# Letting a list scheduler choose each engine's instruction order in a speech-model kernel

## The chip, the cores and the metric

The kernel runs on one core of a Trainium2 chip. The metric is the device time of one execution in microseconds (us). Every kernel here was executed several times beside the kernel before on the same chip. "Ratio" below is the mean time of one kernel's fast runs over the mean of the fast runs of the kernel before in the same rounds, with a 95% interval; so it is not quite the ratio of the medians that are quoted. The kernel gives each of five engines its own sequence of instructions: TensorE (PE, matmuls; PEld is its weight load), VectorE (DVE), ScalarE (ACT), GpSimd (POOL) and SyncE (SP, which issues loads and stores). The kernel makes the engines wait for each other through semaphores.

## The reference

Two strided convolutions with 5 taps, each followed by GELU, then a joint layer (B=2, T=4000, D=512, K=5, U=8):

```python
for i in range(K):
    h = h + einsum("btc,cd->btd", xp[:, i:i+T, :], w1[i])
h = gelu(h)[:, ::2, :]
... the same with w2 on h, giving f[:, ::2, :]        # 1000 frames of each batch
fe = einsum("btd,de->bte", f, w_f);  ge = einsum("bud,de->bue", g, w_g)
j  = tanh(fe[:, :, None, :] + ge[:, None, :, :])
return einsum("btud,dv->btuv", j, w_o)                # (2, 1000, 8, 512)
```

## The kernel before

It is already well tuned: the convolutions use fewer products than the plain form by adding and subtracting inputs and weights first. So TensorE needs *operands* that VectorE and ScalarE make. These are sums and differences of shifted frames (`xt`, `row`, and `xs`, `hT` in place) and of weights (`w_t`). The products are then combined by VectorE (`scalar_tensor_tensor`, in the accumulator `acc` or in `ty`, `sd`), and a ScalarE GELU follows. The frames go through in five tiles of the first convolution, two batches of the second (`Triple`, 4 units each), and then 125 output tiles of 128 rows.

Every operation is recorded once, in program order, and each engine gets its own operations in that order:

```python
for o in ops:                       # program order
    if o.eng != name: continue
    for k, v in o.deps.items(): wait(...)      # latest conflicting op of each other engine
    ins = o.fn(e)
```

The order was placed by hand, as lists of which preparation step follows which product:

```python
LATE = {(0, 0): ((1, "2d"), (0, "next"), (0, "ti"), (0, "t0"), (0, "s0")), (0, 1): ((1, "r"),), ...}
...
def unit(self, m, vec=(), scal=()):            # one output block of a tile
    ... three products; then, in the accumulator:
    for o, f in ((C, 0.5), (Dd, -0.5)):
        stt("dve", ps.cols(o, n), ps.cols(Dd, n), f, c)
    ends.append(end)       # four more products into the same accumulator, then GELU
    finish(2 if m else 1)  # the ends are run one or two units later
```

## Time and profile before

The kernel takes 298.3 us (median of 3; 298.7 with a fourth run).

From the page of the kernel before: span, busy time by engine, rows of busy tenths in 40 slices of the span, and the chain of waits by engine.

```profile
span 296.9 us, 4003 instructions
...
PE 273.6 (92%) x1474; PEld 144.6 (49%) x1486; DVE 188.2 (63%) x282; ACT 172.8 (58%) x220; POOL 1.6 (1%) x18
...
PE   8998699999989959876979869999999999999995
...
DVE  1999956654976973099474322566766767666674
...
PEclk9999799999999989979999979999999999999999
...
PE 66%; DVE 15%; SPq 5%; ACT 5%; DMA 5%; issue 3%; DVEq 0%; ACTq 0%
```

In the PE row the dips lie in slices 5 to 24, so at about 30 to 175 us; from there on, in the output stage, PE never stops. The PEclk row (TensorE's granted clock, in tenths) has four dips that follow the deeper dips of PE. No other engine is near 100% over the span.

The waits of PE in the kernel before: who was waited for, total us, times, longest us.

```profile
PE acc L305 <- DVE hT L294: 3.9, 3, 2.8
PE acc L305 <- ACT jT L298: 3.5, 1, 3.5
PE acc L305 <- DVE acc L447: 2.9, 1, 2.9
PE acc L305 <- issue: 2.7, 1, 2.7
PE acc L305 <- DVE row L294: 2.4, 1, 2.4
PE acc L305 <- DVE feT L778: 1.5, 1, 1.5
...
```

A few long stops, then, not many short ones. What was ahead of the missing operand is seen on the other engines. The timeline of ScalarE of the kernel before, at 121 to 126 us (start, length, engine, line, operation, out<-in, shapes, count, and in brackets the idle time before it and what ended it):

```profile
121.18 3.64 ACT L298 ACTIVATE row<-hT 128x1344 bf16<-128x1344 bf16 x2
124.72 1.30 ACT L298 ACTIVATE row<-row 128x1336 bf16<-128x1336 bf16 x1
```

The timeline of VectorE of the kernel before, just after it:

```profile
126.06 1.62 DVE L294 TENSOR_TENSOR row<-row 128x1336 bf16<-128x1336 bf16 x2 [11.26 <-ACT row L298]
```

The timeline of TensorE of the kernel before, where it waits for that:

```profile
127.74 0.74 PE L305 MATMUL acc<-row,w_sb 128*128 128x334 bf16 x4 [2.37 <-DVE row L294]
```

The copy at 124.72 is what VectorE waits for, and behind VectorE TensorE. It belongs to the first batch. Its input had been there since 103.5 us (end of VectorE's subtract into `row`), but in the list above it stands behind two copies of the second batch, whose input was ready only at 120.7 (end of the last GELU of their tile). So VectorE slept for 11.3 us over a 1.3 us copy.

The half clock is seen in the timeline of TensorE of the kernel before, after the stop of 2.89 us at 29.6 us; four matmuls of 498 columns take 1.87 us in the half-clock stretch and 1.00 us later:

```profile
34.92 1.87 PE L305 MATMUL acc<-xs,w_t 128*128 128x498 bf16 x4
...
41.87 1.00 PE L305 MATMUL acc<-xs,w_t 128*128 128x498 bf16 x4
```

### The profile page before, as it was taken

Reading aid. Unit: us, or ns where it says so; the run is one execution under the profiler, and the core shown is the slowest. Engines: PE = TensorE matmul, PEld = TensorE weight load, DVE = VectorE, ACT = ScalarE, POOL = GpSimd, SP = SyncE. Lnnn points to the kernel's source line nnn. Section 1 sums busy time; section 2 is a strip of 40 time slices with the busy share of each in tenths; the row PEclk is TensorE's granted clock in tenths of the full one; section 3 lists DMA queues with packets and bytes.
Section 4 is the critical chain, followed back from the end, with each engine's and each line's share of the span. In section 5 each row is a group of like instructions: output and inputs, shape, how many; then the busy total and the mean of one; then the engine's idle time right before and its main releaser. Section 6 shows DMA issues by size and latency. Waiting matters only on the chain.

```text
span 296.9 us, 4003 instructions
## 1 busy us (share of the span) xinstructions
PE 273.6 (92%) x1474; PEld 144.6 (49%) x1486; DVE 188.2 (63%) x282; ACT 172.8 (58%) x220; POOL 1.6 (1%) x18
## 2 busy tenths in 40 slices
PE   8998699999989959876979869999999999999995
PEld 4896364444444425544645535444444444444442
DVE  1999956654976973099474322566766767666674
ACT  2758647229328531835442865295976786884941
POOL 1000000000000000000000000000000000000000
PEclk9999799999999989979999979999999999999999
DMA  7999989960000000000000011134444454444444
GB/s 268 279 174 219 203 186 244 348 137 1 2 0 0 2 0 0 0 2 1 0 0 2 0 35 55 53 106 161 145 148 162 135 176 145 156 155 148 159 145 141
DMA packets 54721, 31.87 MB, mean 107 GB/s; under 512 B 31646, under 2 KB 54446, under 8 KB 54702
## 3 DMA queue, kind: packets, MB, share of 16 engines
q1 hardware_dynamic: 54558, 31.55, 38.9%
q8 instruction: 12, 0.20, 0.3%
q10 hardware_dynamic: 144, 0.07, 0.1%
q14 instruction: 7, 0.06, 0.1%
HBM read 7.86 MB, written 16.38 MB: 82 GB/s over the span
## 4 chain that ended last, share of the span: by engine, by line
PE 66%; DVE 15%; SPq 5%; ACT 5%; DMA 5%; issue 3%; DVEq 0%; ACTq 0%
PE acc L305 66%; SPq L337 5%; DVE acc L447 4%; DVE row L294 2%; DMA xs<-in_x_dram 2%; ACT row L298 2%; DVE hT L294 2%; DVE sd L447 2%; DMA w_sb<-in_w_dram 2%; DVE xt L294 1%; DMA xr<-in_x_dram 1%; ACT fT L298 1%; ACT hT L298 1%; DVE xs L294 1%; DVE w_t L294 1%
## 5 line engine op out<-in xcount | busy, mean ns | idle before, releaser
L305 PE MATMUL acc<-wo_sb,jT 128*128 128x512 bf16 (+1 forms) x492 | 109.3, 381 | 4.1 <-ACT jT L298 3.5
L864 DVE CAST ost<-acc 128x512 bf16<-128x512 f32 (+1 forms) x105 | 72.3, 689 | 45.5 <-PE acc L305 45.5
L305 PEld LDWEIGHTS acc<-wo_sb,jT 128*128 128x128 bf16 x504 | 49.7, 99 | 63.2 <-ACT jT L298 3.6
L298 ACT ACTIVATE jT<-feT,geT 128x1000 bf16<-128x1000 f32 (+5 forms) x84 | 70.9, 918 | 0.0
L305 PE MATMUL acc<-xt,w_sb 128*128 128x252 bf16 (+2 forms) x240 | 46.2, 335 | 3.0 <-DVE acc L447 2.9
L298 ACT ACTIVATE hT<-acc 128x996 bf16<-128x996 f32 (+2 forms) x16 | 14.4, 899 | 35.0 <-PE acc L305 35.0
L305 PEld LDWEIGHTS acc<-xt,w_sb 128*128 128x128 bf16 x240 | 23.6, 99 | 20.9 <-ACT cs L298 3.1
L305 PE MATMUL acc<-xs,w_t 128*128 128x498 bf16 (+2 forms) x140 | 30.8, 349 | 1.4 <-DVE xs L294 0.8
L298 ACT ACTIVATE ost<-acc 128x512 bf16<-128x512 f32 (+1 forms) x21 | 12.3, 584 | 29.8 <-PE acc L305 29.8
L447 DVE SCALAR_TENSOR_TENSOR acc<-acc,cs 128x498 f32<-128x498 f32 (+2 forms) x30 | 17.5, 629 | 17.5 <-PE acc L305 10.7
L298 ACT ACTIVATE xt<-xs 128x1992 bf16<-128x1992 bf16 (+2 forms) x14 | 21.6, 1572 | 3.3 <-DMA xs<-in_x_dram 3.3
L305 PE MATMUL acc<-row,w_sb 128*128 128x334 bf16 x96 | 18.7, 320 | 5.1 <-issue 2.7
L305 PE MATMUL acc<-hT,w_t 128*128 128x334 bf16 x96 | 17.2, 317 | 3.9 <-DVE hT L294 3.9
L305 PEld LDWEIGHTS acc<-xs,w_t 128*128 128x128 bf16 x140 | 13.4, 99 | 13.6 <-DVE xs L294 1.5
L305 PE MATMUL acc<-xs,w_sb 128*128 128x252 bf16 (+2 forms) x104 | 19.7, 322 | 0.1
L298 ACT ACTIVATE cs<-acc 128x498 f32<-128x498 f32 (+3 forms) x27 | 12.9, 486 | 10.6 <-PE acc L305 8.5
L298 ACT ACTIVATE fT<-acc 128x334 bf16<-128x334 f32 (+1 forms) x16 | 11.6, 727 | 11.8 <-PE acc L305 11.6
L305 PE MATMUL acc<-xt,w_t 128*128 128x252 bf16 (+2 forms) x88 | 17.4, 329 | 0.0
L294 DVE TENSOR_TENSOR row<-row 128x1336 bf16<-128x1336 bf16 x8 | 6.5, 850 | 16.4 <-ACT row L298 16.4
L305 PE MATMUL acc<-fT,wf_sb 128*128 128x500 bf16 x64 | 14.0, 374 | 1.5 <-DVE feT L778 1.5
L305 PEld LDWEIGHTS acc<-row,w_sb 128*128 128x128 bf16 x96 | 9.5, 101 | 11.0 <-issue 3.1
L294 DVE TENSOR_TENSOR xt<-xt,xs 128x1992 bf16<-128x1992 bf16 (+2 forms) x14 | 14.0, 1011 | 0.4 <-ACT xt L298 0.4
(55 smaller groups left out, 198.4 us busy)
## 6 DMA issues: line engine op xcount, KB each, us to landing
out_dram<-ost SPq DMA_DIRECT2D x109, 128.0 KB, 1.9
w_sb<-in_w_dram SPq DMA_DIRECT2D x10, 512.0 KB, 5.5
xr<-in_x_dram SPq DMA_DIRECT2D x2, 512.0 KB, 3.8
wg_sb<-in_w_g_dram SPq DMA_DIRECT2D x1, 512.0 KB, 10.1
wf_sb<-in_w_f_dram SPq DMA_DIRECT2D x1, 512.0 KB, 6.9
wo_sb<-in_w_o_dram SPq DMA_DIRECT2D x1, 512.0 KB, 7.7
xs<-in_x_dram SPq DMA_TRANSPOSE x16, 4.9
out_dram<-ost SPq DMA_DIRECT2D x2, 120.0 KB
```

Source lines behind the costliest of these rows:

```text
L294: pl.op(eng, lambda e: e.tensor_tensor(out=o.ap, in0=a.ap, in1=b.ap, op=op), (a, b), (o,))
L298: pl.op("act", lambda e: e.activation(o.ap, i.ap, func, scale=scale, bias=0.0 if bias is None else bias.ap), rd, (o,))
L305: ins = e.matmul(o.ap, lhsT=l.ap, rhs=r.ap, start=start and n == 0, stop=stop and n == len(pairs) - 1, skip_group_check=not check)
L337: pl.dma("sp", lambda e: e.dma_start_transpose(out=dst.ap, in_=src), (), (dst,))
L447: pl.op(eng, lambda e: e.scalar_tensor_tensor(out=o.ap, in0=a.ap, scalar=f, in1=b.ap, op0=ALU.mult, op1=add), (a, b), (o,))
L864: pl.op("dve", lambda e, o=o, v=v: e.tensor_copy(out=o.ap, in_=v.ap), (v,), (o,))
```

## The change

Its intent is that instruction order is no longer written by hand but computed at build time: a list scheduler walks through simulated time with a cost for each operation and a model of the loads, and each engine takes an operation that is ready. On VectorE and ScalarE it is the one that TensorE will need soonest (`late`, worked out backwards from TensorE's own sequence). On TensorE, SyncE and GpSimd it is the first in program order of those that are ready, so TensorE too may go round a product whose operands aren't there. The result is a fixed order per engine. The opening, up to the second tile's operands, stays pinned to program order. Three further outputs of the second tile are moved from `unit` to the form that keeps its sums apart (`whole` and `post`), which costs an extra VectorE add each.

```diff
+    def edges(self):      # all pairs of ops that touch the same bytes or PSUM bank
+    ...
+    def schedule(self, pred):
+        for i in range(n - 1, -1, -1):
+            t = min([late[s] - (HOP if pred[s][i] else ...) for s in succ[i]], default=0.0)
+            if ops[i].eng == "pe":
+                t = min(t, nextpe)
+            late[i] = t - span[i]
+    ...
+            now = [i for i in cand[e] if ready[i] <= t + 0.02]
+            i = min(now, key=(lambda i: i) if e in ("pe", "sp", "pool") else (lambda i: (late[i], i)))
+    ...
+            if o.dma:
+                wire = max(wire, t + 1.0) + o.nbytes / 222e3
+                end = max(wire, t + 2.0)
 ...
-            for o in ops:
-                if o.eng != name:
-                    continue
+            for i in order[name]:
 ...
+        def vec_cost(o, ins, fast=True):
+            return o.ap.free_size() * (0.52e-3 if bf else 1.04e-3) + 0.065
 ...
-        post0(1)
-        post0(2, (lambda: tiles[2].shift("a0"),))
-        post0(3)
-        tiles[2].xf("a0")
-        t1.post(0, t1.whole(0), (lambda: tiles[2].shift("b1"),))
-        tiles[2].xf("a1")
+        pl.pin = False
+        for m in base0:
+            post0(m)
+        ... all operands of the third tile
+        for m in range(WHOLE):          # 4; was 1
+            t1.post(m, t1.whole(m))
```

No matmul, load, store or eviction is added or saved, apart from the three adds.

More of the change, by code (lines that the diff above doesn't have):

```diff
@@ L63 @@
 class Op:
-    __slots__ = ("eng", "fn", "deps", "dma", "signal", "count", "sem", "val", "idx")
+    __slots__ = ("eng", "fn", "reads", "writes", "dma", "signal", "count", "sem", "val", "idx", "cost", "pin", "after", "nbytes")
 class Plan:
     COMPUTE = ("pe", "act", "dve", "pool")
+    HOP = 0.16
     def __init__(self, nc):
@@ L74, in __init__ @@
         self.ops = []
-        ncell = 229376 // CELL + 1
-        z = lambda n: {e: np.full(n, -1, np.int64) for e in self.COMPUTE + ("dma",)}
-        self.lw, self.lr, self.pa = z(ncell), z(ncell), z(8)
-    def _deps(self, eng, reads, writes):
-        need = {}
-        def add(e, arr, cells):
-            m = int(arr[cells].max())
-            if m >= 0:
-                if e == "dma":
-                    for d in set(arr[cells].tolist()):
-                        if d >= 0:
-                            need[("dma", d)] = True
-                else:
-                    need[e] = max(need.get(e, -1), m)
-        for v in list(reads) + list(writes):
-            if v.psum:
-                for e in self.COMPUTE:
-                    if e != eng:
-                        add(e, self.pa[e], v.cells)
-        for v in reads:
-            if not v.psum:
-                for e in self.lw:
-                    if not (e == eng == "pe"):
-                        add(e, self.lw[e], v.cells)
-        for v in writes:
-            if not v.psum:
-                for e in self.lw:
-                    if not (e == eng == "pe"):
-                        add(e, self.lw[e], v.cells)
-                        add(e, self.lr[e], v.cells)
-        return need
@@ L110, in op @@
-    def op(self, eng, fn, reads=(), writes=()):
+        self.pin = True
+    def op(self, eng, fn, reads=(), writes=(), cost=0.1):
         o = Op()
         o.eng, o.fn, o.dma, o.signal, o.idx = eng, fn, False, False, len(self.ops)
-        o.deps = self._deps(eng, reads, writes)
+        o.reads, o.writes, o.cost, o.pin, o.after = tuple(reads), tuple(writes), cost, self.pin, []
         self.ops.append(o)
-        for v in list(reads) + list(writes):
-            if v.psum:
-                self.pa[eng][v.cells] = o.idx
-        for v in reads:
-            if not v.psum:
-                self.lr[eng][v.cells] = o.idx
-        for v in writes:
-            if not v.psum:
-                self.lw[eng][v.cells] = o.idx
@@ L124, in op, with dma @@
         return o
-    def dma(self, eng, fn, reads=(), writes=(), sem=None):
+    def dma(self, eng, fn, reads=(), writes=(), sem=None, nbytes=524288):
         o = Op()
         o.eng, o.fn, o.dma, o.signal, o.idx = eng, fn, True, False, len(self.ops)
-        o.deps = self._deps("dma_issue", reads, writes)
+        o.reads, o.writes, o.cost, o.pin, o.after, o.nbytes = tuple(reads), tuple(writes), 0.05, True, [], nbytes
         if sem is None:
@@ L135, in dma @@
         self.ops.append(o)
-        for v in reads:
-            self.lr["dma"][v.cells] = o.idx
-        for v in writes:
-            self.lw["dma"][v.cells] = o.idx
-        return o
+        return o
+    def edges(self):
+        ops = self.ops
+        sets, label = {}, {False: np.zeros(229376 // CELL + 1, np.int64), True: np.arange(8)}
+        for o in ops:
+            for v in o.reads + o.writes:
+                k = (v.psum, v.cells.tobytes())
+                if k not in sets:
+                    sets[k] = v.cells
+                    if not v.psum:
+                        lab = label[False]
+                        lab[v.cells] += lab.max() + 1
+                        label[False] = np.unique(lab, return_inverse=True)[1]
+        na = int(label[False].max()) + 1
+        atoms = {k: (np.unique(label[k[0]][c]) + (na if k[0] else 0)) for k, c in sets.items()}
+        R = np.zeros((len(ops), na + 8), np.float32)
+        W = np.zeros_like(R)
+        for o in ops:
+            for m, vs in ((R, o.reads), (W, o.writes)):
+                for v in vs:
+                    m[o.idx, atoms[(v.psum, v.cells.tobytes())]] = 1
+        sb = slice(0, na)
+        hit = lambda s: (W[:, s] @ (R + W)[:, s].T + R[:, s] @ W[:, s].T) > 0
+        sbuf, psum = hit(sb), hit(slice(na, na + 8))
+        pred = []
+        last = {}
+        for o in ops:
+            p = {}
+            for j in np.flatnonzero(sbuf[o.idx, :o.idx] | psum[o.idx, :o.idx]).tolist():
+                q = ops[j]
+                if o.dma and q.dma and not set(x for v in o.writes for x in v.cells.tolist()) & set(
+                        x for v in q.reads + q.writes for x in v.cells.tolist()):
+                    continue
+                same = q.eng == o.eng and not q.dma and not o.dma
+                over = any(W[o.idx, c] > R[o.idx, c] and R[j, c] + W[j, c] > 0 for c in range(na, na + 8))
+                p[j] = not same or (bool(sbuf[o.idx, j] or over) and o.eng != "pe")
+            for j in o.after:
+                p[j] = True
+            if o.pin:
+                j = last.get(o.eng)
+                if j is not None:
+                    p.setdefault(j, False)
+                last[o.eng] = o.idx
+            pred.append(p)
+        return pred
@@ new lines, in schedule @@
+    def schedule(self, pred):
+        ops, HOP = self.ops, self.HOP
+        n = len(ops)
+        succ = [[] for _ in ops]
+        for i, p in enumerate(pred):
+            for j in p:
+                succ[j].append(i)
+        span = [o.cost + (4.0 if o.dma else 0.0) for o in ops]
+        late, nextpe = [0.0] * n, 0.0
+        for i in range(n - 1, -1, -1):
+            t = min([late[s] - (HOP if pred[s][i] else ops[i].cost - span[i]) for s in succ[i]], default=0.0)
+            if ops[i].eng == "pe":
+                t = min(t, nextpe)
+            late[i] = t - span[i]
+            if ops[i].eng == "pe":
+                nextpe = late[i]
+        left = [len(p) for p in pred]
+        ready = [0.0] * n
+        free = {e: 0.0 for e in ("pe", "act", "dve", "pool", "sp")}
+        cand = {e: [] for e in free}
+        for i in range(n):
+            if not left[i]:
+                cand[ops[i].eng].append(i)
+        order = {e: [] for e in free}
+        wire, start = 0.0, [0.0] * n
+        for _ in range(n):
+            best = None
+            for e, c in cand.items():
+                if c:
+                    t = max(free[e], min(ready[i] for i in c))
+                    if best is None or t < best[0]:
+                        best = (t, e)
+            t, e = best
+            now = [i for i in cand[e] if ready[i] <= t + 0.02]
+            i = min(now, key=(lambda i: i) if e in ("pe", "sp", "pool") else (lambda i: (late[i], i)))
+            cand[e].remove(i)
+            order[e].append(i)
+            o = ops[i]
+            start[i] = t
+            free[e] = t + o.cost
+            end = free[e]
+            if o.dma:
+                wire = max(wire, t + 1.0) + o.nbytes / 222e3
+                end = max(wire, t + 2.0)
+            for s in succ[i]:
+                ready[s] = max(ready[s], end + HOP if pred[s][i] else free[e])
+                left[s] -= 1
+                if not left[s]:
+                    cand[ops[s].eng].append(s)
+        self.start = start
+        self.end = max(free.values())
+        return order
@@ L142, in emit @@
     def emit(self, block, tail):
         nc, ops = self.nc, self.ops
+        pred = self.edges()
+        order = self.schedule(pred)
+        pos = {i: p for e in order for p, i in enumerate(order[e])}
+        deps = []
         for o in ops:
-            for k, v in o.deps.items():
+            need = {}
+            for j, w in pred[o.idx].items():
+                q = ops[j]
+                if not w:
+                    continue
+                if q.dma:
+                    need[("dma", j)] = j
+                elif q.eng not in need or pos[need[q.eng]] < pos[j]:
+                    need[q.eng] = j
+            deps.append(need)
+            for k, j in need.items():
@@ L146, in emit @@
                 if not isinstance(k, tuple):
-                    ops[v].signal = True
+                    ops[j].signal = True
         cnt = {e: 0 for e in self.COMPUTE}
         sem = {e: nc.alloc_semaphore(f"s_{e}") for e in self.COMPUTE}
-        for o in ops:
-            if not o.dma:
-                if o.signal:
-                    cnt[o.eng] += 1
-                o.count = cnt[o.eng]
+        for e in self.COMPUTE:
+            for i in order[e]:
+                if not ops[i].dma:
+                    if ops[i].signal:
+                        cnt[e] += 1
+                    ops[i].count = cnt[e]
@@ L162, in wait @@
                     e.wait_ge(s, v)
-            for o in ops:
-                if o.eng != name:
-                    continue
-                for k, v in o.deps.items():
+            for i in order[name]:
+                o = ops[i]
+                for k, j in sorted(deps[i].items(), key=lambda kj: -kj[1]):
                     if isinstance(k, tuple):
-                        wait(ops[k[1]].sem, ops[k[1]].val)
+                        wait(ops[j].sem, ops[j].val)
                     else:
-                        wait(sem[k], ops[v].count)
+                        wait(sem[k], ops[j].count)
                 ins = o.fn(e)
@@ L237, in bass_standalone__seq2seq_rnn_t_joint__speech_kernel @@
     NWARM = 10
+    WHOLE = 4
     with ExitStack() as es:
@@ L288, in bass_standalone__seq2seq_rnn_t_joint__speech_kernel @@
         sub, add = ALU.subtract, ALU.add
+        def vec_cost(o, ins, fast=True):
+            bf = fast and all(not v.psum and v.ap.dtype == BF16 for v in (o,) + tuple(ins))
+            return o.ap.free_size() * (0.52e-3 if bf else 1.04e-3) + 0.065
         def memset(v):
@@ L293, in tt @@
         def tt(eng, o, a, b, op):
-            pl.op(eng, lambda e: e.tensor_tensor(out=o.ap, in0=a.ap, in1=b.ap, op=op), (a, b), (o,))
+            pl.op(eng, lambda e: e.tensor_tensor(out=o.ap, in0=a.ap, in1=b.ap, op=op), (a, b), (o,),
+                  vec_cost(o, (a, b)))
         def act(o, i, func, scale=1.0, bias=None):
@@ L298, in act @@
             pl.op("act", lambda e: e.activation(o.ap, i.ap, func, scale=scale,
-                                                bias=0.0 if bias is None else bias.ap), rd, (o,))
+                                                bias=0.0 if bias is None else bias.ap), rd, (o,),
+                  o.ap.free_size() * 0.83e-3 + 0.11)
         def mm(o, pairs, start, stop, check=True):
@@ L307, in fn @@
                 return ins
-            pl.op("pe", fn, [v for pr in pairs for v in pr], (o,))
+            pl.op("pe", fn, [v for pr in pairs for v in pr], (o,), len(pairs) * max(o.ap.free_size() / 2400 + 0.0025, 0.1))
         zv = zero[:]
@@ L344, in load_w1 @@
             if after is not None:
-                o.deps[("dma", after.idx)] = True
+                o.after.append(after.idx)
             return o
@@ L374, in fn @@
                     return ins
-                pl.op("pe", fn, (xr[rt][:], ident[:]), (pv,))
+                pl.op("pe", fn, (xr[rt][:], ident[:]), (pv,), 0.8)
                 o = xs[0][pp::2, :, 16 + rt * P:16 + (rt + 1) * P]
@@ L379, in bass_standalone__seq2seq_rnn_t_joint__speech_kernel @@
                 else:
-                    pl.op("dve", lambda e, o=o, pv=pv: e.tensor_copy(out=o.ap, in_=pv.ap), (pv,), (o,))
+                    pl.op("dve", lambda e, o=o, pv=pv: e.tensor_copy(out=o.ap, in_=pv.ap), (pv,), (o,), vec_cost(o, (pv,)))
         def shift(src, off, dst, c0, n, which):
@@ L447, in stt @@
             pl.op(eng, lambda e: e.scalar_tensor_tensor(
-                out=o.ap, in0=a.ap, scalar=f, in1=b.ap, op0=ALU.mult, op1=add), (a, b), (o,))
+                out=o.ap, in0=a.ap, scalar=f, in1=b.ap, op0=ALU.mult, op1=add), (a, b), (o,),
+                  vec_cost(o, (a, b), False))
         def w2part(m, part):
@@ L735, in bass_standalone__seq2seq_rnn_t_joint__speech_kernel @@
         t1.xf("a3")
-        post0(1)
-        post0(2, (lambda: tiles[2].shift("a0"),))
-        post0(3)
-        tiles[2].xf("a0")
-        t1.post(0, t1.whole(0), (lambda: tiles[2].shift("b1"),))
-        tiles[2].xf("a1")
+        pl.pin = False
+        for m in base0:
+            post0(m)
+        nxt = tiles[2]
+        nxt.shift("a0")
+        nxt.xf("a0")
+        nxt.shift("b1")
+        nxt.xf("a1")
+        nxt.shift("a3")
+        for w in ("a2", "b1", "b3", "a3"):
+            nxt.xf(w)
+        for m in range(WHOLE):
+            t1.post(m, t1.whole(m))
         flush()
@@ L777, in fe @@
                     else:
-                        pl.op("dve", lambda e, o=o, v=v: e.tensor_copy(out=o.ap, in_=v.ap), (v,), (o,))
+                        pl.op("dve", lambda e, o=o, v=v: e.tensor_copy(out=o.ap, in_=v.ap), (v,), (o,), vec_cost(o, (v,)))
         def tanh(v, k):
@@ L805, in bass_standalone__seq2seq_rnn_t_joint__speech_kernel @@
             nx = tiles[qi + 1] if qi + 1 < len(tiles) else None
-            for m in range(1 if qi == 1 else 0, NK):
+            for m in range(WHOLE if qi == 1 else 0, NK):
                 if qi == 1:
-                    scal = ((), ("a3",), (), ())[m]
-                    vec = ((), ("a2", "b1"), ("b3", "a3"), ())[m]
+                    scal, vec = (), ()
                 elif nx:
@@ L863, in bass_standalone__seq2seq_rnn_t_joint__speech_kernel @@
                 else:
-                    pl.op("dve", lambda e, o=o, v=v: e.tensor_copy(out=o.ap, in_=v.ap), (v,), (o,))
+                    pl.op("dve", lambda e, o=o, v=v: e.tensor_copy(out=o.ap, in_=v.ap), (v,), (o,), vec_cost(o, (v,)))
                 lo = c0
@@ L871, in bass_standalone__seq2seq_rnn_t_joint__speech_kernel @@
                     dst = out[b, t:t + n, u, cl]
-                    pl.dma(("sp", "act")[h], lambda e, src=src, dst=dst: e.dma_start(dst, src.ap), (src,), (), slot_sem[s])
+                    pl.dma(("sp", "act")[h], lambda e, src=src, dst=dst: e.dma_start(dst, src.ap), (src,), (), slot_sem[s], 2 * n * P * 4)
                     lo += n
```

## The prediction

> **What bounds the kernel now.** TensorE. The page shows PE 92% busy (273.6 of 296.9 us); the chain of waits has 66% on PE. The output stage (from 173 us) is gapless in the timeline: nothing is to be had there. What a reordering can win lies between 24 and 173 us, where PE stands still though its operands could have been made earlier. The PE timeline shows these idle stretches: 2.9 us at 29.6 (vector work of the second tile's units), 0.8 at 81.7 (a subtract queued behind weight sums), 2.7 + 0.8 at 105 to 109, 2.4 at 125.3 and 2.8 + 0.3 at 137.7 to 142 (operands of the second convolution), 1.5 at 154 (feT evictions), 3.5 at 169.5 (first tanh rows). With crumbs at 24 to 29 that is about 19 us.
>
> **The clock.** After four of them (29.6, 105, 125, 169.5) matmuls run at half speed for about 3.4 us (498 columns take 0.41 us between starts instead of 0.21; granted clock 0.83 in 30 to 40 us). [...] Each costs 1.7 us, together 7. Removable in all: about 25 us.
>
> **Order or data?** Mostly order. VectorE is 69% busy from 40 to 110 us, ScalarE less. At 126 VectorE had waited 11.3 us for a ScalarE copy standing behind the other batch's copies (3.6 us). The tanhs at 165 to 173 use feT that was ready at 160. The scheduler puts what TensorE needs soonest first, and lets PE take whichever product is ready. What it can't lift: 20 to 40 us, where VectorE is busy 19.4 of 20 us and x arrives until 30.8; and the second convolution, where VectorE needs 2.4 us per unit and 10 us of operands per batch against 5.0 us of PE per unit, nearly as much as PE, and the second batch's operands can't start before their buffer is free at 119.7.
>
> **Added.** Three more outputs of the second tile take the separate path: each adds a 504-column add (0.68 us), 2 us of VectorE in its fullest stage, but PE then needn't wait for VectorE in mid-accumulation. The scheduler's costs are 10 to 20% below the trace (0.60 against 0.69 us for 512 f32 on VectorE; 0.94 against 1.12 for a tanh), and it counts the half-size loads of x as full ones, so it expects x some 5 us late and puts other work ahead. New small PE gaps will come of this. No matmul or byte is saved.
>
> **Sum (gain, with clock).** 24 to 40 us: 3.5 of 6.5; 81: 0.7; 105: 4.5 of 5.1; 125: 3.5 of 4.1; 138: 1.5 of 3.1; 154: 1; 169: 4.5 of 5.2. That is 19; less 1.5 for new gaps: 17.5.
>
> **Predicted: 280.8 us, 274 to 290 in 8 of 10. Faster by over 2%: 0.91; within 2%: 0.07; slower: 0.02.**
>
> **What would show it.** PE busy falls to 265 to 272 us (less half clock) while its share rises to 95% or more. The dips of the PE clock row near 33, 108, 129 and 173 us go, at most one staying. The output stage keeps its length and starts about 17 us sooner. PE's waits for jT and row vanish; one for VectorE near 22 to 35 us remains.
>
> **What would make it wrong.** A static order from wrong costs can stall in-order engines: VectorE behind a late product, or tanhs ahead of an eviction in the output stage. If the second convolution is truly bound by VectorE, 125 to 140 gains little and the time is near 288.

## The result and the profile after

The changed kernel takes 273.5 us (median of 4; 273.3 to 274.2) against 298.7 us: ratio 0.9172 (0.9132 to 0.9212). It is 25.1 us faster; 17.5 had been predicted, and the time lies just below the stated range.

From the page of the changed kernel, the same lines:

```profile
span 271.7 us, 3949 instructions
...
PE 265.2 (98%) x1474; PEld 142.7 (53%) x1486; DVE 188.5 (69%) x285; ACT 173.6 (64%) x220; POOL 1.6 (1%) x18
...
PE   8899999999999999999999999999999999999995
...
DVE  1899999829999952699544354666667656657764
...
PEclk9999999999999999999999999999999999999999
...
PE 87%; ACT 6%; DMA 4%; issue 1%; SPq 0%; DVE 0%
```

The dips are gone from both the PE row and the clock row. VectorE does the same work (188.5 against 188.2 us), only sooner: its row is now at 8 or 9 tenths in slices 2 to 8 and 10 to 14, where it had holes in slices 6 to 10, 12 and 13; one hole is left, in slice 9. All that is left of PE's waits:

```profile
PE acc L383 <- DVE zero L390: 1.2, 1, 1.2
PE acc L383 <- DVE xt L370: 0.7, 1, 0.7
PE acc L383 <- ACT fT L375: 0.6, 1, 0.6
PE acc L383 <- ACT hT L375: 0.3, 1, 0.3
```

Two of these are in the pinned opening (the first at the very start, the 0.7 us at 7.2 us); between 20 us and the end PE stands still for 0.8 us. The copy that had been queued wrongly now runs soon after the two copies (and the subtract) that it depends on, 35.7 us earlier in the run; in the timeline of ScalarE of the changed kernel:

```profile
81.75 3.65 ACT L375 ACTIVATE row<-hT 128x2688 bf16<-128x2688 bf16 x2
...
89.04 1.31 ACT L375 ACTIVATE row<-row 128x1336 bf16<-128x1336 bf16 x1
...
109.96 3.65 ACT L375 ACTIVATE row<-hT 128x2688 bf16<-128x2688 bf16 x2
```

The copies of the second batch follow at 109.96, when their input exists.

The account of the 25.2 us between the two spans (all sums worked out from the PE timelines and the clock records; PE idle is without the 3.1 us after the last matmul, the same in both):

| | before | after | difference |
|---|---|---|---|
| PE idle, all | 20.3 | 3.5 | 16.8 |
| half-clock stretches (four of 3.41 us, less 0.55 us of a stop that lies in one; half of the rest is lost) | 6.5 | 0 | 6.5 |
| rest (PE's busy time) | | | 1.9 |

Part of the rest is most likely the end of the last matmul before a stop, which the trace counts as busy: a group of four 498-column matmuls ends 1.00 us after its start, but the next group starts 0.84 us after it when there is one, so each stop hides about 0.16 us more. There are ten stops before and three after, so that is 1.1 us of the 1.9. This is an estimate from those two numbers and was not tested; the other 0.8 us is not accounted for. The output stage, from its fourth tile on, is as long as before: the span between the second block of output matmuls (181.65 us before, 156.41 after) and the last matmul (293.9 and 268.7) is 112.2 us in both.

### The profile page after: what moved, and what is told of

Same layout as the page of the kernel before. It is cut to its first block, busy times and chain, and to the rows that moved or that the text cites. A ratio compares the mean times of both kernels' runs of the same rounds, so it can differ in the third digit from the quotient of the medians.

```text
span 271.7 us, 3949 instructions
## 1 busy us (share of the span) xinstructions
PE 265.2 (98%) x1474; PEld 142.7 (53%) x1486; DVE 188.5 (69%) x285; ACT 173.6 (64%) x220; POOL 1.6 (1%) x18
## 4 chain that ended last, share of the span: by engine, by line
PE 87%; ACT 6%; DMA 4%; issue 1%; SPq 0%; DVE 0%
PE acc L383 87%; DMA w_sb<-in_w_dram 4%; ACT jT L375 3%; ACT fT L375 1%; ACT cs L375 0%; ACT xt L375 0%; ACT feT L375 0%; SPq L407 0%; DVE feT L864 0%; ACT hT L375 0%; ACT ost L375 0%
## 5 line engine op out<-in xcount | busy, mean ns | idle before, releaser
L383 PE MATMUL acc<-wo_sb,jT 128*128 128x512 bf16 (+1 forms) x492 | 107.8, 377 | 1.2 <-ACT fT L375 0.6
L375 ACT ACTIVATE jT<-feT,geT 128x1000 bf16<-128x1000 f32 (+10 forms) x84 | 72.1, 922 | 17.9 <-PE acc L383 16.9
L383 PE MATMUL acc<-xs,w_t 128*128 128x498 bf16 (+2 forms) x140 | 29.5, 341 | 0.0
L375 ACT ACTIVATE hT<-acc 128x996 bf16<-128x996 f32 (+2 forms) x13 | 12.6, 967 | 21.0 <-PE acc L383 21.0
L525 DVE SCALAR_TENSOR_TENSOR sd<-acc,cs 128x334 f32<-128x334 f32 x16 | 7.4, 500 | 18.3 <-PE acc L383 15.3
L383 PEld LDWEIGHTS acc<-xs,w_t 128*128 128x128 bf16 x140 | 13.6, 98 | 10.9
L383 PE MATMUL acc<-row,w_sb 128*128 128x334 bf16 x96 | 17.5, 305 | 0.0
L383 PE MATMUL acc<-hT,w_t 128*128 128x334 bf16 x96 | 16.3, 305 | 0.0
L525 DVE SCALAR_TENSOR_TENSOR acc<-acc,cs 128x498 f32<-128x498 f32 (+1 forms) x24 | 15.3, 678 | 0.8 <-PE acc L383 0.8
L383 PEld LDWEIGHTS acc<-xs,w_sb 128*128 128x128 bf16 x104 | 10.0, 98 | 7.2 <-DVE xs L458 0.9
```

What stands on the lines that cost most here:

```text
L375: pl.op("act", lambda e: e.activation(o.ap, i.ap, func, scale=scale, bias=0.0 if bias is None else bias.ap), rd, (o,), o.ap.free_size() * ...
L383: ins = e.matmul(o.ap, lhsT=l.ap, rhs=r.ap, start=start and n == 0, stop=stop and n == len(pairs) - 1, skip_group_check=not check)
L525: pl.op(eng, lambda e: e.scalar_tensor_tensor(out=o.ap, in0=a.ap, scalar=f, in1=b.ap, op0=ALU.mult, op1=add), (a, b), (o,), vec_cost(o, (a ...
```

## The experiments

In all of them the numbers to compare with are 273.5 us and ratio 0.9172 for the changed kernel, and 298.4 to 299.2 us for the kernel before. All 15 gave correct results.

### Which engine's freedom does it?

Four kernels with the program text of before, built by the new class. `HOLD` lists the engines that stay in program order:

```diff
+    HOLD = ("pe", "act", "dve", "pool")      # old_all_held; 3, 1 or 0 of them in the others
-        ... cost, self.pin, []
+        ... cost, self.pin or eng in self.HOLD, []
```

> Program text of before (second tile mostly by in-place units), with the new dependence bookkeeping, but every engine held to program order. Theory (the gain is order): within 1.5 us of before, about 298. Rival (the new pairwise dependences drop waits that the old bookkeeping had): below 293.

Measured: 298.5 us, ratio 1.003 (0.997 to 1.008). The new bookkeeping of dependences by itself is worth nothing. PE stops at the same ten places.

> As old_all_held, but TensorE alone is freely ordered; VectorE, ScalarE and GpSimd stay in program order. Theory (the operands come late because VectorE and ScalarE make them in the wrong order): little gain, 293 to 297. Rival (TensorE taking whatever product is ready fills its own gaps): below 285.

Measured: 279.6 us, ratio 0.937 (0.933 to 0.942). The theory fell: TensorE's own freedom gives three quarters of the gain, with VectorE and ScalarE in the old order. Its PE waits for VectorE and ScalarE after the start sum to 5.4 us, and no half-clock stretch is left within the work of the profiled run (two of the other three executions have a mean clock of 0.993 to 0.994, so probably one stretch). The old 3.5 us wait for the first tanh rows is gone because PE now does most of the last products of the second convolution in that time, which the old text had placed behind the third output tile. The first output matmuls in the timeline of TensorE of the kernel before:

```profile
173.05 4.22 PE L305 MATMUL acc<-wo_sb,jT 128*128 128x512 bf16 x11 [3.51 <-ACT jT L298]
177.11 0.73 PE L305 MATMUL acc<-row,w_sb 128*128 128x334 bf16 x4
```

The same in the timeline of old_pe_free, with products of the second convolution right before them:

```profile
157.55 0.73 PE L383 MATMUL acc<-hT,w_sb 128*128 128x334 bf16 x4
158.17 2.76 PE L383 MATMUL acc<-wo_sb,jT 128*128 128x512 bf16 x12
```

> TensorE held to program order; VectorE, ScalarE and GpSimd freely ordered. Theory: most of the gain, 277 to 284, what is missing lies at 24 to 40 us. Rival (TensorE's own choice does it): 290 or more.

Measured: 277.5 us, ratio 0.930 (0.927 to 0.933). As expected. What is missing lies at 21 to 37 us: small stops for VectorE of 0.2 to 1.3 us and, in the profiled run (278.2 us, clock 0.994), one half-clock stretch. The other three executions have a clock of 1.000 and take 277.3 to 277.5 us, so most of the median's distance is the stops.

> All engines freely ordered, program text of before, so the changed kernel without its three further separate outputs of the second tile. Theory: 275 to 278, the separate outputs are worth 2 to 4 us at 24 to 40 us because TensorE then need not wait for VectorE in mid-accumulation. Rival (the scheduler alone does all): within 1 us of the changed kernel, 273.5.

Measured: 274.5 us, ratio 0.920 (0.917 to 0.923). This is within 1 us of the changed kernel, and the intervals overlap, so the three further separate outputs are worth at most about 1 us, not 2 to 4; the trace shows 0.7 us of stops at 22 to 26 us that the changed kernel hasn't.

What follows: the two freedoms are substitutes. Singly they gain 18.8 and 21 us, together 24. A stop of PE goes away when the operand comes sooner, or when PE has something else that is ready; here one of the two was mostly enough.

### Does urgency matter?

```diff
-            i = min(now, key=(lambda i: i) if e in ("pe", "sp", "pool") else (lambda i: (late[i], i)))
+            i = min(now, key=lambda i: i)
```

> The changed kernel, but VectorE and ScalarE take the ready instruction that is first in program order, as TensorE does; the urgency is not used. Theory A (urgency towards TensorE is what fills the gaps): 277 to 283. Theory B (after the first four runs: either side's freedom is enough, so any order by readiness does): within 1.5 us of the changed kernel, below 275.

Measured: 274.5 us, ratio 0.920 (0.917 to 0.924). Theory B: taking the first ready operation in program order does nearly as well; the difference of 0.3% is inside the intervals. "Ready" is what counts here, "most urgent" adds at most about 1 us. Not tested is how much of the gain moving the few misplaced steps by hand would have brought.

### How good must the cost model be?

The prediction deducted 1.5 us for errors of the scheduler's costs. `true_cost` mends them; the three flat kernels make them much worse.

```diff
 # true_cost
-            return o.ap.free_size() * (0.52e-3 if bf else 1.04e-3) + 0.065
+            return o.ap.free_size() * (0.52e-3 if bf else 1.04e-3) + 0.155
-                  o.ap.free_size() * 0.83e-3 + 0.11)
+                  o.ap.free_size() * 0.83e-3 + (0.28 if bias is not None else 0.17))
 # loads of x: nbytes = (hi - lo) * 1024 instead of 524288 for all
 # flat_cost: both of these; flat_compute: the first alone; flat_load: the second alone
+        for o in ops:
+            if not o.dma: o.cost = 0.7
+            else:         o.nbytes = 0
```

> The changed kernel, with the scheduler's costs of VectorE and ScalarE raised to the durations of the trace (0.69 us for 512 f32, 1.11 for a tanh of 1000) and the loads of x counted at their true size. The prediction held 1.5 us for gaps that wrong costs make: ratio to the changed kernel 0.994. Rival (TensorE stands only 0.8 us between 21 and 268 us, so nothing is left): within 0.3% of the changed kernel, 273 to 274.

Measured: 273.2 us, ratio 0.916 (0.913 to 0.919). Nothing beyond noise. The errors that the prediction listed (10 to 20% on VectorE and ScalarE, 5 us on the loads of x) cost next to nothing.

> The changed kernel, but the scheduler believes that every compute instruction and group of matmuls takes 0.7 us and every load lands 2 us after issue. Theory A (the order is only as good as its cost model, as the prediction feared): 280 or more. Theory B (the operands have so much slack that a rough order will do): below 277.

Measured: 294.7 us, ratio 0.988 (0.984 to 0.992). Five sixths of the gain are gone. The PE timeline of this kernel at its longest stop:

```profile
32.64 1.84 PE L388 MATMUL acc<-xt,w_sb 128*128 128x252 bf16 x8 [10.88 <-ACT hT L380]
```

The ScalarE timeline of this kernel, in the time of that stop:

```profile
25.45 3.63 ACT L380 ACTIVATE xt<-xs 128x1992 bf16<-128x1992 bf16 x2 [6.08 <-DMA xs<-in_x_dram]
30.16 1.86 ACT L380 ACTIVATE xt<-xs 128x1992 bf16<-128x1992 bf16 x1 [1.07 <-DMA xs<-in_x_dram]
31.93 0.57 ACT L380 ACTIVATE hT<-acc 128x504 bf16<-128x504 f32 x1
```

The 504-column GELU of the first tile at 31.93, which frees an accumulator bank for PE, stands behind copies of the *third* tile's x, which the scheduler took for loaded. ScalarE sits before them waiting for the load, 6.08 and 1.07 us, and doesn't go round it; PE stands for 10.9 us and then runs at about half speed (the eight 252-column matmuls after the stop take 1.84 us, eight at 38.43 us in the kernel before 1.02 us at a granted clock of 1.00).

> As flat_cost, but only the compute costs are flat (0.7 us each); the model of the loads is the changed kernel's. If wrong durations spoil the order: 282 or more. If flat_cost was lost through its loads alone (order that puts work on a late load ahead of work that is ready, on engines that can't go round it): below 277.

> As flat_cost, but only the loads are made to land 2 us after issue; compute costs are the changed kernel's. If wrong durations did it: below 277. If the loads did it: 283 or more, with TensorE standing some 10 us near 22 us as in flat_cost, behind a ScalarE copy of the third tile that waits for x.

Measured: flat_compute 288.1 us, ratio 0.962 (0.953 to 0.971); flat_load 280.0 us, ratio 0.938 (0.932 to 0.943). Both halves of the cost model are needed: 14.6 and 6.5 us over the changed kernel, by medians, which happens to make the 21.1 us of flat_cost. For flat_load neither branch had the number right: the stop near 22 us is there, behind the same kind of copy, but it is 3.7 us, not 10, with 6.8 us of half clock, of which 5.6 us lie in the work and cost about 2.8. In flat_compute PE stops at 25.0 (2.9 us), 43.8 (1.5), 48.0 (3.1), 128 (1.8) and 162 us (2.3). So a fixed order bears errors of a tenth or two, but not a model that takes all operations (0.1 to 2.4 us each in the traces) for equal or loads for immediate.

### Is the second convolution nearly bound by VectorE?

The prediction said so and kept back 1.6 of the 3.1 us there. More of VectorE's work, to no purpose, tests it:

```diff
                 stt("dve", s, P_(bm), 0.5, c)
+                stt("dve", s, P_(bm), 0.5, c)      # extra1: once more; extra3: three times more
```

> The changed kernel, with one VectorE instruction of each of the 8 units of the second convolution done twice (same values, about 0.5 us each, 4 us in all); the scheduler knows of it. If the second convolution is nearly bound by VectorE, as the prediction said: 3 to 4 us longer than the changed kernel, 276.5 to 277.5. If the order leaves slack (VectorE busy 29.7 of the 50 us from 100 to 150): under 0.7 us longer.

> As extra1, but the instruction is done four times (12 us more of VectorE in the second convolution). Nearly bound: 10 us longer or more, 283 or more. Slack: less than 4 us longer, below 277.5, with gaps of TensorE only where the doses fill the stage of 110 to 130 us (VectorE busy 8.8 of 10).

Measured: extra1 273.7 us, ratio 0.916 (0.911 to 0.922); extra3 274.5 us, ratio 0.919 (0.914 to 0.924). The added instructions last 12 us one by one in extra3; as they overlap a little with their neighbours (in the changed kernel one of 0.50 us starts at 122.88 us and the next instruction at 123.30), VectorE's busy time rises by 9.6 us (198.1 against 188.5), of which 8.7 us lie between 100 and 150 us. Of this about 1 us shows in the time. In the changed kernel the stage is not bound by VectorE.

### Does a full VectorE bind the stage from 20 to 50 us?

```diff
-                for s, f in ((0, 0.5), (1, -0.5)):
+                for s, f in ((0, 0.5), (1, -0.5)) * 2:      # in post, 7 outputs
```

> The changed kernel, with the two VectorE instructions that combine the products of each of the 7 separately kept outputs of the first two tiles done twice (14 times 0.37 us, 5.2 us more of urgent VectorE work between 20 and 41 us, where VectorE is busy 99%). If a full VectorE binds this stage, as the prediction said: 4 to 5 us longer than the changed kernel, 278 or so. If what fills VectorE there is mostly work that can wait (operands of later tiles): under 1.5 us longer, below 275.

Measured: 274.6 us, ratio 0.918 (0.914 to 0.922): about 1 us. The added instructions last 5.2 us one by one; VectorE's busy time rises by 4.3 us (192.8 against 188.5). The stretch from 20 to 50 us, as start and end, length, then busy us and instruction count of PE, PEld, DVE, ACT and POOL, the clock, the DMA share and GB/s; the first line is the kernel before, the second the changed kernel, the third extra_posts, each in its own fence:

```profile
20.00:50.00 30.00, 26.34 (x176) 17.12 (x174) 23.66 (x38) 20.38 (x24) 0.17 (x1) 0.94 1.03 206
```

```profile
20.00:50.00 30.00, 29.74 (x205) 19.47 (x203) 29.42 (x47) 23.89 (x28) 0.17 (x1) 1.00 1.13 208
```

```profile
20.00:50.00 30.00, 28.55 (x195) 18.13 (x194) 30.00 (x57) 23.98 (x28) 0.17 (x1) 1.00 1.10 209
```

VectorE is busy 29.4 of 30 us in the changed kernel and PE still gets 29.7; with VectorE at 30.0 PE loses 1.2 us, not 4 to 5. An engine can be full because it has work to do ahead. In this stage it was the operands of the fourth tile, which PE touches from 51 us on; urgent work goes before it and pushes it back. In extra_posts VectorE makes these operands (2016 columns) at 46 to 58 us, in the changed kernel at 41 to 52, and what gives way is its idle time behind them (4.8 us before 59.9 us in the changed kernel, 2.0 us before 62.0 us in extra_posts).

### Do the stages gain separately?

`first_half` is the changed kernel with everything from the second convolution on pinned again. `second_half` is the reverse, with the program text of before.

```diff
+        pl.pin = True          # first_half;  pl.pin = False in second_half, which starts pinned
         for b in range(B):     # the second convolution
```

> The changed kernel, but every instruction from the second convolution on is held to program order among its like; only the first convolution is freely ordered. If the stages gain separately: the gaps at 125, 138, 154 and 169 us stay (13.9 us with the clock), so 287 to 288. If a free first part feeds the second part early enough anyway: below 281.

Measured: 287.2 us, ratio 0.960 (0.955 to 0.965). As expected. The four later stops stay at nearly their old lengths; two of them, from the PE timeline of first_half:

```profile
116.65 0.74 PE L383 MATMUL acc<-row,w_sb 128*128 128x334 bf16 x4 [2.37 <-DVE row L370]
129.22 0.74 PE L383 MATMUL acc<-hT,w_t 128*128 128x334 bf16 x4 [2.57 <-DVE hT L370]
```

The kernel before had 2.37 us there too, and 2.78.

> The program text of before, the first convolution held to program order, the second convolution and all after it freely ordered. If the stages gain separately: 298.5 less 13.9, so 284 to 286, and the gains of first_half and second_half add up to 25. If the two overlap: their sum is well over 25.

Measured: 280.5 us, ratio 0.937 (0.933 to 0.942), 4 us better than if the stages were apart. Its PE timeline still has the stop of the first part (3.7 us at 29.7, with a half-clock stretch), and 0.7 us at 82.6; but of the 2.7 + 0.8 us and the half clock at 105 to 109 only 0.9 us is left. That stop lies at the seam: the freed side could pull the last products of the first convolution ahead of it or make the operands sooner (which of the two did it was not taken apart), and both kernels all but remove it. By ratios, on the 299.2 us of this call, the two gain 12.0 and 18.8 us, 30.8 together, 6 more than the whole change; the 5.1 us of the stop at the seam, less the 0.9 that remains, is most of that.

### What is the clock worth by itself?

Idle matmuls in two of the old stops keep TensorE busy and make nothing ready sooner:

```diff
+        def fill(bk, n):       # matmuls with zero weights into a bank that the next product starts anyway
+            for _ in range(n): mm(ps.cols(bk * NT, NT), [(zero[0:P], w2_sb[0, 0])], True, True)
+                if self.b == 0 and m == 0: fill(b1, 12)       # before the first product of the second convolution
+        fill(banks[0], 16)                                     # before the first output tile
```

> The kernel before, with 12 idle matmuls of 512 columns (2.6 us) ahead of the first product of the second convolution and 16 (3.4 us) ahead of the first output tile, into the bank that the next product starts afresh, so in two of the idle stretches (2.7 and 3.5 us) and nowhere else. No operand comes sooner. Theory (half of the loss at such a gap is the clock that the idle time takes away): both half-clock stretches go and 1.7 us each with them, ratio 0.987 to 0.991, 295 us. Rival (the clock follows something else, or the fillers delay the work): ratio 0.997 to 1.01.

Measured: 297.2 us, ratio 0.9965 (0.9915 to 1.0016): the theory's 0.987 to 0.991 was missed, and the interval doesn't tell whether there is any gain. In the profiled execution the fillers work as meant: the half-clock stretches at 108.6 and 173.4 us are gone, two are left, and the run took 295.7 us. But other executions of the same kernel have other mean clocks, and the time goes with it: 294.8 us at clock 0.994, 295.7 to 297.3 at 0.988, 299.0 and 299.1 at 0.983. One half-clock stretch more or less moves the mean clock by 0.0057 (1.7 us of 297), so by this estimate these are one, two and three stretches, and each costs about 2 us. The runs of the kernel before show the same: 296.7 us at 0.983, 297.1 at 0.981, 298.3 to 300.0 at 0.975 to 0.977. At equal clock the filled kernel is about 2 us slower than before (299 against 296.7 at 0.983), which was not explained: no trace of such a run was looked at. So runs of one kernel that differ in clock agree with the size of the clock term (1.7 us each), though other things may differ between them too, and the comparison of the two kernels stays open.

## Why the prediction was right or wrong

**Right: the bound and the list of stops.** TensorE bound the kernel, the output stage had nothing to give (112.2 us in both), and the removable time was put at about 25 us, of which about 19 standing still and 7 clock. The changed kernel gained 25.1. That the totals agree so closely is in part luck: of the two parts that were listed, 16.8 and 6.5 us came, and 1.9 us of PE's busy time, which was not listed, came in addition.

**Right: order, not data.** Of the ten stops, 18.3 us in all, 0.8 us is left after 20 us. PE's busy time fell to 265.2 us and its share rose to 98%; all four clock dips went. The output stage starts 25 us sooner, where about 17 was said.

**Wrong: the amount kept back.** The step that failed is what the sum kept back, "That is 19; less 1.5 for new gaps: 17.5", and behind it above all the claim that VectorE limits the two stages at 20 to 40 us and in the second convolution. Of 26.3 us of stage terms 7 were kept back and then 1.5 more; the runs show that almost none of it stayed, and that VectorE limits neither stage. Term by term:

- *24 to 40 us, "3.5 of 6.5".* The first product of the fourth tile came at 56.15 us before and 51.00 after, 5.15 us sooner. The reasons given for keeping 3 us back were that VectorE is busy 19.4 of 20 us there and that x arrives until 30.8 us (a wait of VectorE for x, of 0.19 us, ends at 30.84 us; this was not tested by itself). That VectorE is full is true (29.4 of 30 us from 20 to 50 us, against 23.7 before); that it binds is false in the changed kernel (extra_posts: 4.3 us more busy time, 1 us more time).
- *138 us, "1.5 of 3.1".* All 3.1 came. "Nearly as much as PE" was a wrong count: it put the operands of both batches into the stage, though in the changed kernel most of the first batch's are made while PE is still on the first convolution (from 82 us on; PE's first product of the second is at 98.7), and it left the fT products out of PE's side. From 100 to 150 us VectorE is busy 29.7 of 50 us; 9.6 us more busy time in all cost 1 us (extra3).
- *105, 125, 154, 169 us.* 13.5 of 15.9 us predicted; 15.3 came, 0.6 us of a stop remains at 150 us.
- *New gaps, "1.5".* There is 0.8 us of stops after 20 us, and mended costs bring nothing measurable (true_cost). The fear was right in kind (flat_cost, flat_compute and flat_load lose 6 to 21 us of the 25), but far off for errors of 10 to 20%.
- *The second tile's separate outputs* were seen as a trade of VectorE time against a freer PE; they are worth at most about 1 us either way (old_all_free).

**Not foreseen.** The prediction told of TensorE's freedom in half a sentence. It alone gives 18.8 us. With two ways to close most stops, each of which alone brings three quarters of the gain or more, there was little reason to keep back a share of each stage: both ways would have to fail there.

**The clock.** In the kernel before, the granted clock is 0.50 in four stretches of 3.41 us (from 33.50, 108.59, 129.07 and 173.45 us), and each comes after a stop of PE: of 2.89, 2.68, 2.37 and 3.51 us. The stop of 2.78 us before 140.51 us was not followed by one (granted clock 1.00 from 132.5 to 173.4 us), so here the length of a stop alone does not tell whether the clock is lost too; what else decides was not shown. In flat_load, with the stop of 3.7 us near 22 us, the half clock lasted 6.8 us (granted clock 0.69 from 20 to 30 us and 0.97 from 30 to 40). How many stretches there are also varies between executions of one kernel: one to three in before_filled, judged by the mean clock (0.983 to 0.994; 299 to 295 us).

## What to carry to other kernels

Where a bound engine stands still a few times for 2 to 4 us while the others have room, first ask what stood in the queue ahead of the missing operand; if it is work that could wait, nearly all of the idle time may come back, as it did here (16.8 of 20.3 us), and the half clock after it too (6.5 us). A full engine need not bind a stage: in the stage tested here only its *urgent* work counted (4.3 us more busy time cost 1 us), so count that, not the busy share. A fixed order computed at build time bore costs that were wrong by a tenth or two, but it needed real durations (14.6 us) and a model of when loads land (6.5 us): in flat_cost ScalarE waited 6.1 and 1.1 us for x with a GELU behind it, and PE stood 10.9 us for that GELU.
